# Attention and two MoE layers on one core: heads taken in pairs from the ninth unit on, the second batch's v sums moved to VectorE, and a re-costed planner

## The chip, the cores and the metric

The kernel runs on one core of one Trainium2 chip. The metric is the device time of one execution in microseconds (us), lower is better. An execution of this kernel is compared with another by the median of several runs; a profiled execution gives the trace.

## The reference

Inputs are q, k and v of shape (2 batches, 8 heads, 768 positions, 64) in float32, and four weight matrices in float64.

```python
k_sum = k.reshape(B, H, nb, block, D).max(axis=3)      # block = 32, so 24 blocks
v_sum = v.reshape(B, H, nb, block, D).mean(axis=3)
scores_l = scale * q @ k.T, kept where |i - j| < 16, else -1e9
scores_s = scale * q @ k_sum.T + log(32)
a = softmax(concat(scores_l, scores_s))                # a / (sum + 1e-9)
attn = a @ concat(v, v_sum)
x = attn as (1536 tokens, 512)
h = x @ w_in;  x = (h * clip(h + 3, 0, 6) / 6) @ w_out     # first MoE layer, 512 -> 2048 -> 512
h = x @ w_in2; out = (h * cos(h)) @ w_out2                 # second MoE layer
```

So each query sees at most 31 neighbours of its own and 24 block summaries, and the attention output is the token matrix of the first MoE layer. The host only lays the inputs out (transposed q and k with 16 columns of padding, v cut into windows of 96 rows).

## The kernel before, in words

**Attention.** A unit is one pair of heads (they share the 128 partitions, 64 each), one batch and 256 queries: `HT` = 2 tiles of 128. There are 24 units: 2 batches x 3 query thirds (`h`) x 4 pairs (`p`). A unit (`att`, L505) does the following. TensorE makes the scores in 8 small matmuls of 64x64 stationary elements (`score`, L515) into the two PSUM banks `s`, against a window of 96 keys and the 24 block maxima (120 columns, `CE`). VectorE adds the mask and takes the minimum in four instructions (L529), ScalarE takes four exponentials with their sums (L537), GpSimd adds 1e-9 (L546), VectorE inverts (L551) and GpSimd or VectorE scales (L555). TensorE transposes four 128x120 pieces into bank `t` (L564), ScalarE or VectorE copies them to `pt`, and TensorE multiplies by v in 8 small matmuls (`pv`, L573) into bank `o`. The result goes to SBUF as `xh` and the remainder `xl` (L580 and L582, by helpers at L403 and L410).

The k maxima are VectorE reductions (`k_prep`, L497). The v block means are made on TensorE: `vsum_pe` (L470) runs twelve matmuls of 96x32 stationary elements against the constant `avg` (L477), copies the bank to `y`, adds the four row groups with one more matmul (L482), copies the 24 rows to `vs`, and `fill` (L489) spreads them over the 12 windows of `vw`.

The score matmuls, the v product, and both matmuls of the v sums use tiles of the TensorE array (64x64, 120x64, 96x32, 128x32). All other matmuls, the transposes among them, use the array whole.

**MoE.** Weights arrive as float64 numbers, two 32-bit words each, and are unpacked by ScalarE, VectorE and GpSimd into a high and a low part (`weights`, L609). `g1` (L657) computes h for a chunk of 128 hidden columns: 3 matmuls for each of 4 slices of the model dimension (L667 to L669); `post` (L676) makes the activation with its high and low part; `g2` (L726) accumulates the output (L743). A block is 512 tokens and 4 chunks; the first block is cut into two halves of 256 tokens. In all there are 192 MoE matmuls of 256 columns and 2208 of 512.

**Who sets the order.** `Plan` (L121) is a list scheduler that runs when the kernel is built. Every operation has the engines that may do it with a cost on each, a priority, and what it reads, writes and takes. `order` (L243) plays the program with these costs, always gives a free engine the ready operation of lowest priority number, and so fixes the order on each of TensorE, ScalarE, VectorE, GpSimd and the one DMA queue of SyncE. On the chip these orders are fixed programs: an engine waits at an instruction until what it reads is there, with all later ones behind it. The planner's costs are never seen by the chip. Priorities come from the table `T` (L77): `A0` and `AS` set the start and spacing of the units, `g0` and `gi` those of the MoE chunks, and others move a load or a preparation ahead. `refine` (L223) repeats the plan with due times.

```python
    units += [(b, h, p) for b in range(B) for h in range(NH) for p in range(NP) if b or h > 1]
    for y, (b, h, p) in enumerate(units):
        pr = A0 + AS * HT * y
        ...
        att(b, h, p, kws[p], z, vws[p], pr, c_s)
```

Of the kernel before, what the change touches and what calls it, by code (L numbers as in the profile page):

```python
# [11 lines left out]
F32 = mybir.dt.float32  # L12
# [6 lines left out]
P = 128  # L19
# [28 lines left out]
def layout(q, k, v, moe_w_in, moe_w_out, moe2_w_in, moe2_w_out):  # L48
# [5 lines left out]
    qt, kt = (pair(x).transpose(0, 1, 2, 4, 3).reshape(B, NP, P, S) for x in (q, k))  # L54
# [5 lines left out]
    return dict(q=qt, k=kt, v=vw, w_in1=w_in[0], w_out1=w_out[0], w_in2=w_in[1], w_out2=w_out[1])  # L60


def consts():
# [14 lines left out]
    A0=6.982, AS=1.584, mask=-12.92, kp=-20.41, qp=-33.47, lk=-17.33, lq=-11.81, lv=-4.43, vs=33.64, vss=-16.92,  # L78
    vsp=-29.27, wl=-1.64, wc=-25.07, g0=20.77, gi=7.33, pp=27.42, fill=-9.73, DVE=1.348, POOL=0.497, cold=5, d0=0.9,
    warm=9, tail=1, lagq=1, nraw=3, ncf=2, n=5, w2=2, n2=3, g2=3, nz=3, busy=0, slack=0.2, vpe=-7.47, avg=-27.4,  # L80
# [36 lines left out]
class Op:  # L117
    __slots__ = ("engs", "fn", "prio", "port", "seq", "wait", "after", "ready", "takes", "uses", "start", "eng", "took")


class Plan:  # L121


    AFTER = {"PE": 0.2, "ACT": 0.135, "DVE": 0.13, "POOL": 0.09, "DMA": 0.95}
    TO_PE = {"PE": 0.0, "ACT": 0.2, "DVE": 0.19, "POOL": 0.15, "DMA": 0.95}
# [6 lines left out]
    def op(self, engs, fn, prio, r=(), w=(), take=(), port=0.0):  # L132
        o = Op()
        o.engs, o.fn, o.prio, o.port, o.seq = engs, fn, prio, port, len(self.ops)
# [49 lines left out]
    def deadlines(self, order):  # L184
# [17 lines left out]
        for o in reversed(order):  # L202
            t = end
            for a in o.after:
                t = min(t, late[id(a)] - (self.TO_PE if a.eng == "PE" else self.AFTER)[o.eng])
            for x in o.uses:
                if id(x) in follow and id(follow[id(x)]) in late:
                    t = min(t, late[id(follow[id(x)])] - self.AFTER[o.eng])
# [33 lines left out]

    def order(self):  # L243
# [5 lines left out]
        moved = self.end = 0.0  # L249
# [13 lines left out]
        while events:  # L263
# [11 lines left out]
            for e in names:  # L275
# [29 lines left out]
                cost = o.engs[e] * (2.0 if e == "PE" and now < T["cold"] else 1.0)  # L305
                if e == "DVE" and free["POOL"] > now + 0.1:
                    cost += o.port
# [3 lines left out]
                if e == "DMA":  # L311
                    moved = max(moved, now + 1.1) + cost
                    end, free[e] = moved, max(now + 0.52, moved - 2.5)
                    self.end = max(self.end, end + 1.3)
                else:
                    free[e] = end
                    self.end = max(self.end, end)
                push(free[e], "free", None)
                if o.seq < self.first:
                    first -= 1  # L320
                    opens = max(opens, end + self.AFTER[e])
                    if not first:
                        push(opens, "turn", None)
                for a in o.after:
                    a.ready = max(a.ready, end + (self.TO_PE if "PE" in a.engs else self.AFTER)[e])
# [3 lines left out]
                for x in o.uses:  # L329
                    x.uses -= 1  # L330
                    if not x.uses:
                        push(end + self.AFTER[e], "release", x)
# [4 lines left out]
    def run(self):  # L337
        self.refine()
        left, last, spare = self.first, T["cold"], True
        for o in self.order():  # L340
            if o.eng == "PE":
                if spare and last < T["busy"]:
                    for _ in range(int((o.start - last - T["slack"]) / (0.11 if last > T["cold"] else 0.22))):
                        self.idle()
                last = o.start + o.took
                spare = spare and not any(x.cls is self.spare and x.slot == 1 for x in o.uses)
# [8 lines left out]
def body(ctx: ExitStack, tc: tile.TileContext, q, k, v, w_in1, w_out1, w_in2, w_out2, ident_d, mask_d, avg_d, out):  # L355
# [13 lines left out]
    avg = ap.tile([P, AW + QD], F32, name="avg")  # L369
# [5 lines left out]
    part01 = [[cp.tile([P, TOK], F32, name=f"part{j}{m}") for m in range(KT)] for j in range(2)]  # L375
    c_z = slots("z", T["nz"], [P, HT * P], pool=ap)
    c_vw = slots("vw", 4, [P, NS, P], pool=ap)
    c_vs = slots("vs", 2, [P, P], pool=ap)
    c_y = slots("y", 1, [P, P], pool=ap)
# [53 lines left out]
    pl.spare = c_acc  # L433
    pl.idle = lambda: nc.tensor.matmul(out=c_acc.tiles[1][:, 0:SUB], lhsT=ident, rhs=ident[:, 0:SUB], start=True, stop=True)
# [6 lines left out]
    def load_consts():  # L441
        dma(lambda: mask[:, 1, :], lambda: mask_d, 0.34, T["mask"], w=["mask"])

# [9 lines left out]
    def load_q(b, h, p, prio):  # L453
        z = Buf(c_z)
        dma(lambda: z.t, lambda: q[b, p][:, HT * P * h:HT * P * h + HT * P], 0.54, prio, w=[z], take=[z])
        return z

    def load_k(b, p, prio):
# [3 lines left out]
            2.45, prio, w=[(kw, "own")], take=[kw])  # L462
        return kw, ks

    def load_v(b, p, prio):
        vw = Buf(c_vw)
        dma(lambda: vw.t[0:CW, :, :], lambda: v[b, p], 1.75, prio, w=[(vw, 0)], take=[vw])
        return vw

    def vsum_pe(vw, prio):  # L470

        bank, x, y = Buf(c_h), Buf(c_vs), Buf(c_y)

        def mm(e):
            for s in range(NS):
                a, g = 2 * (NS - 1 - s), s % 4 * QD
                nc.tensor.matmul(out=bank.t[g:g + QD, 0:P], lhsT=avg[0:CW, a:a + QD], rhs=vw.t[0:CW, s, :],  # L477
                                 start=(s < 4), stop=(s >= NS - 4), tile_position=(0, g))

        op({"PE": 0.85}, mm, prio, r=["avg", (vw, 0)], w=[bank], take=[bank, x, y])  # L480
        op({"ACT": 0.2, "DVE": 0.2}, lambda e: copy(e, y.t, bank.t[:, 0:P]), prio, r=[bank], w=[y])
        op({"PE": 0.25}, lambda e: nc.tensor.matmul(out=bank.t[CW:P, P:2 * P], lhsT=avg[:, AW:AW + QD], rhs=y.t,  # L482
# [341 lines left out]
```

## Time and profile before

| | |
|---|---|
| median of 3 runs | 609.16 us (608.8 to 609.82) |
| span of the profiled execution, first to last instruction | 605.7 us |
| what lies around the span, by the median | 3.5 us |
| TensorE (PE) busy | 590.8 us, 98% of the span |
| VectorE, ScalarE, GpSimd busy | 385.7, 268.5, 346.9 us (64%, 44%, 57%) |
| chain that ended last | PE 92%, all else 1 to 2% each |
| bytes read from HBM | 46.31 MB, mean 83 GB/s |

The page gives the span of the profiled execution and no separate end-to-end time, so the time of that execution is taken as its span and the 3.5 us around it. A busy share of PE counts each matmul from its start to its modelled end, and matmuls overlap; how fast PE really goes is read from the distance between the starts of its instructions in the timeline.

### The profile page before, as it was taken

The page shows a single profiled execution, that of the slowest core. Times are in us where ns is not written, and L with a number is a line of the kernel's source. Part 1 is how long each engine was busy: PE and PEld are TensorE (multiplying, and loading weights), DVE is VectorE, ACT ScalarE, POOL GpSimd, SP SyncE. Part 2 cuts the span into 40 slices and gives each one's busy share as a digit, 9 for nine tenths or more (in the row PEclk, how much of TensorE's full clock was granted, in tenths as well). Part 3 has the DMA queues.
Part 4 walks back from the last instruction along what each step waited for, and adds up shares of the span by engine and source line. Part 5 has one row for each costly group of instructions (what it writes and reads, how often), then busy time and mean ns, then how long its engine had stood idle before and what let it go on. Part 6 is the DMA issues. An engine that isn't in the chain of part 4 may idle for free.

```text
span 605.7 us, 9370 instructions
## 1 busy us (share of the span) xinstructions
PE 590.8 (98%) x3490; PEld 484.6 (80%) x3490; DVE 385.7 (64%) x724; ACT 268.5 (44%) x585; POOL 346.9 (57%) x366
## 2 busy tenths in 40 slices
PE   5889999999999999999999999999999999999997
PEld 4568787788888888888888888888888888888886
DVE  3699994433942259523982689857984897574562
ACT  3788896533421214201440546654662363343240
POOL 2677774645843537524688398655863577443340
PEclk9999999999999999999999999999999999999999
DMA  9979940122410014200530013302330030000112
GB/s 229 291 232 296 249 137 12 35 105 70 139 70 0 1 42 149 90 0 1 170 108 0 1 70 106 104 2 73 101 104 2 0 105 0 2 0 1 70 44 95
DMA packets 28333, 50.05 MB, mean 83 GB/s; under 512 B 14464, under 2 KB 17920, under 8 KB 28288
## 3 DMA queue, kind: packets, MB, share of 16 engines
q1 hardware_dynamic: 28144, 49.40, 26.9%
q8 instruction: 27, 0.44, 0.3%
q14 instruction: 18, 0.15, 0.1%
q10 hardware_dynamic: 144, 0.07, 0.0%
HBM read 46.31 MB, written 3.15 MB: 82 GB/s over the span
## 4 chain that ended last, share of the span: by engine, by line
PE 92%; DVE 2%; POOL 2%; DMA 1%; ACT 1%; issue 1%; SPq 0%; DVEq 0%; POOLq 0%; ACTq 0%
PE acc L743 25%; PE s L743 18%; PE h L667 8%; PE h L668 8%; PE h L669 8%; PE o L668 3%; PE t L668 3%; PE o L669 3%; PE t L669 3%; PE t L667 3%; PE o L667 3%; PE s L515 2%; PE t L564 2%; PE o L573 2%; DVE cf L627 1%; DMA z<-in_q_dram 1%
## 5 line engine op out<-in xcount | busy, mean ns | idle before, releaser
L405 POOL TENSOR_SCALAR g<-r 128x512 fp32r<-128x512 f32 (+1 forms) x81 | 61.9, 764 | 135.4 <-DVE r L703 40.7
L410 POOL TENSOR_TENSOR g<-r,g 128x512 fp32r<-128x512 f32 (+1 forms) x73 | 100.5, 1377 | 7.3 <-ACT g L403 2.8
L699 ACT ACTIVATE n<-h,bias 128x512 f32<-128x512 f32 (+1 forms) x60 | 39.4, 656 | 142.1 <-PE h L669 140.0
L743 PE MATMUL acc<-g,w 128*128 128x512 f32 (+1 forms) x432 | 96.1, 370 | 0.0
L667 PE MATMUL h<-xh,w 128*128 128x512 f32 (+1 forms) x240 | 92.4, 385 | 0.0
L668 PE MATMUL h<-xl,w 128*128 128x512 f32 (+1 forms) x240 | 90.1, 375 | 0.6 <-DVE xl L410 0.6
L669 PE MATMUL h<-xh,w 128*128 128x512 f32 (+1 forms) x240 | 89.9, 375 | 0.0
L743 PEld LDWEIGHTS acc<-g,w 128*128 128x128 f32 x432 | 75.3, 188 | 14.3 <-issue 0.8
L703 DVE SCALAR_TENSOR_TENSOR r<-n,h 128x512 f32<-128x512 f32 (+1 forms) x60 | 38.7, 646 | 56.8 <-ACT n L699 31.1
L743 PE MATMUL acc<-w,g 128*128 128x512 f32 x288 | 69.2, 389 | 0.0
L743 PE MATMUL s<-w,g 128*128 128x512 f32 x288 | 69.2, 389 | 0.0
L410 POOL TENSOR_TENSOR w<-cf,w 128x512 fp32r<-128x512 f32 x44 | 63.9, 1456 | 3.3 <-ACT w L403 1.6
L743 PEld LDWEIGHTS acc<-w,g 128*128 128x128 f32 x288 | 54.1, 188 | 11.2
L743 PEld LDWEIGHTS s<-w,g 128*128 128x128 f32 x288 | 54.0, 188 | 11.2
L627 DVE SCALAR_TENSOR_TENSOR cf<-cu,cf 128x512 uint32<-128x512 uint32 x64 | 60.0, 955 | 0.4
L618 ACT ACTIVATE cu<-raw 128x512 f32<-128x512 f32 x64 | 42.9, 670 | 38.2 <-DVE cf L627 23.6
L622 DVE TENSOR_SCALAR cf<-raw 128x512 uint32<-128x512 uint32 x64 | 46.6, 744 | 11.8 <-POOL w L410 11.6
L667 PEld LDWEIGHTS h<-xh,w 128*128 128x128 f32 x240 | 45.1, 188 | 10.0 <-issue 1.7
L711 POOL TENSOR_SCALAR n<-n 128x512 f32<-128x512 f32 x45 | 31.5, 700 | 37.6 <-ACT n L699 37.6
L668 PEld LDWEIGHTS h<-xl,w 128*128 128x128 f32 x240 | 45.1, 188 | 8.5 <-DVE xl L410 0.8
L669 PEld LDWEIGHTS h<-xh,w 128*128 128x128 f32 x240 | 45.1, 188 | 8.2
L405 POOL TENSOR_SCALAR w<-cf 128x512 fp32r<-128x512 f32 x41 | 31.4, 771 | 30.3 <-DVE cf L627 23.2
(93 smaller groups left out, 1025.9 us busy)
## 6 DMA issues: line engine op xcount, KB each, us to landing
raw<-in_w_in_dram SPq DMA_DIRECT2D x32, 512.0 KB, 4.1
raw<-in_w_out_dram SPq DMA_DIRECT2D x32, 512.0 KB, 3.8
kw<-in_k_dram SPq DMA_DIRECT2D x8, 576.0 KB, 5.7
vw<-in_v_dram SPq DMA_DIRECT2D x8, 576.0 KB, 9.0
z<-in_q_dram SPq DMA_DIRECT2D x24, 128.0 KB, 5.9
out_dram<-part SPq DMA_DIRECT2D x8, 256.0 KB, 2.0
out_dram<-kw SPq DMA_DIRECT2D x3, 256.0 KB, 2.0
out_dram<-kw SPq DMA_DIRECT2D x2, 128.0 KB, 1.7
```

The lines of the kernel that those rows point to most:

```text
L405: eng[e].tensor_scalar(out=out, in0=in_, scalar1=scale, scalar2=0.0, op0=ALU.mult, op1=ALU.add)
L410: eng[e].tensor_tensor(out=out, in0=in0, in1=in1.bitcast(F32), op=ALU.subtract)
L618: lambda e, raw=raw, u=u: nc.scalar.activation(out=u.t, in_=raw.t.bitcast(F32)[:, :, 1], func=ACTF.Prelu, scale=2.0 ** -112, alpha=2.0 ** 32),
L622: lambda e, raw=raw, f=f: eng[e].tensor_scalar(out=f.t.bitcast(U32), in0=raw.t[:, :, 0], scalar1=2.0 ** -29, scalar2=7.0, op0=ALU.mult, op ...
L627: lambda e, u=u, f=f: nc.vector.scalar_tensor_tensor(out=f.t.bitcast(U32), in0=u.t.bitcast(U32), scalar=3, in1=f.t.bitcast(U32), op0=ALU.l ...
L667: nc.tensor.matmul(out=o, lhsT=wh, rhs=hi, start=(kk == 0), stop=False)
L668: nc.tensor.matmul(out=o, lhsT=wh, rhs=lo, start=False, stop=False)
L669: nc.tensor.matmul(out=o, lhsT=wl, rhs=hi, start=False, stop=(kk == KT - 1))
L699: op({"ACT": t(fixed, 0.43)}, lambda e: nc.scalar.activation(out=out(), in_=in_(), func=func, **kw), pr, r=rd, w=wr, take=take)
L703: op({"DVE": t(0.09, 0.56)}, lambda e: nc.vector.scalar_tensor_tensor(out=out(), in0=a(), scalar=s, in1=b(), op0=o0, op1=o1), pr, r=rd, w= ...
L711: op({"POOL": t(0.16, 0.47), "DVE": t(0.07, 0.265)}, lambda e: eng[e].tensor_scalar(out=n(), in0=n(), scalar1=1.0, scalar2=-MAGIC, op0=ALU ...
L743: nc.tensor.matmul(out=o, lhsT=l, rhs=r, start=(c == 0 and z == 0), stop=(c == GS - 1 and z == 2))
```

## The change

Four things are changed.

1. **Pairs.** The units of the last third of batch 0 and all of batch 1 (from the ninth unit on) are taken two pairs of heads at a time: eight double units. One score run makes the scores of both (16 small matmuls in a row, columns 0 to 239 and 240 to 479 of the same two banks), the softmax and transposes stay one pair at a time, and one `pv` run multiplies both by v, with one `xh` and one `xl` evacuation of twice the width.
2. **v sums of batch 1.** The host also passes v transposed (`vt`). For batch 1 it is loaded into `y` (128x768), VectorE sums groups of 32 (new `tensor_reduce`), TensorE transposes the 24 columns back, and the copy to `vs` scales by 1/32. The twelve matmuls and the one after them are gone for these four pairs; batch 0 keeps them.
3. **Planner.** Costs are changed; an entry into a tiled mode costs 0.15 more, a PE operation that was only just ready costs more, PE costs double while a modelled clock is slow, and VectorE and GpSimd delay each other by a modelled lock. A new step `nudge` moves priorities at random, with 25 fixed seeds.
4. **The table `T`.** Among others A0 from 6.982 to -22.127, AS from 1.584 to 1.369, g0 from 20.77 to 40.246, gi from 7.33 to 11.932 and pp from 27.42 to 80.856.

```diff
+NUDGES = (301016, 301018, ...)
-            op({"PE": 0.58}, score, prio,
+        op({"PE": 0.17 + 0.4 * n}, score, prio, mode=1,
-    def vsum_pe(vw, prio):
+    def v_sums(b, p, prio):
         bank, x, y = Buf(c_h), Buf(c_vs), Buf(c_y)
+        if b:
+            dma(lambda: y.t, lambda: vf[b - 1, p], 1.15, prio + T["lvt"], w=[y], take=[y])
+            op({"DVE": 0.86},
+               lambda e: nc.vector.tensor_reduce(
+                   out=x.t[:, CW:CE], in_=y.t.rearrange("p (c j) -> p c j", j=BLK), axis=AX.X, op=ALU.add),
+               prio, r=[y], w=[(x, 2)], take=[x])
+            op({"PE": 0.11}, lambda e: nc.tensor.transpose(out=bank.t[0:CE, 0:P], in_=x.t[:, 0:CE], identity=ident),
+               prio, r=[(x, 2)], w=[bank], take=[bank])
+            op({"ACT": 0.172, "DVE": 0.215}, lambda e: copy(e, x.t[CW:CE, :], bank.t[CW:CE, 0:P], 1.0 / BLK), prio,
+               r=[bank], w=[(x, 0), (x, 1), (x, 2)])
+            return x
...
         def score(e):
+            for x, p in enumerate(ps):
+                for i, u, o in subs:
+                    nc.tensor.matmul(
+                        out=sp[o].t[u * SUB:u * SUB + SUB, x * W + i * CE:x * W + i * CE + CE], ...)
...
         def pv(e):
+            for x, p in enumerate(ps):
+                for i, u, o in subs:
+                    f = slice(D * o, D * o + D)
+                    a, c = (2 * i + o) * P + u * SUB, (x * HT + i) * P + u * SUB
+                    nc.tensor.matmul(out=res.t[f, c:c + SUB], lhsT=vws[b, p].t[0:CE, 2 * (HT * h + i) + u, f],
+                                     rhs=pts[x].t[0:CE, a:a + SUB], start=True, stop=True)
...
-    units += [(b, h, p) for b in range(B) for h in range(NH) for p in range(NP) if b or h > 1]
+    units = [(b, h, (p,)) for b, h, p in units]
+    units += [(b, h, (p, p + 1)) for b in range(B) for h in range(NH) for p in range(0, NP, 2) if b or h > 1]
...
+    for x in c_vs.tiles:
+        nc.gpsimd.memset(x, 0.0)
...
+                if e == "PE":
+                    while tick_at <= now:
+                        slow, busy, tick_at = self.clock(slow, busy), 0.0, tick_at + self.WATCH
+                    cost *= 2.0 if slow else 1.0
+                    if o.mode and not mode:
+                        cost += 0.15
```

What this does to the order on the engines is shown at three places. The first is TensorE in the middle of the attention, where the v sums of batch 1 stand. Before (`avg` marks the v sums, `pt` the v product, `ident` the transposes, the rest is MoE):

```order
L743 MATMUL acc_130<-g_126,w_116 128x256 x3
L477 MATMUL h_133<-vw_89,avg 32x128 x12
L564 MATMUL t_134<-ident,e_102 120x128 x4
L667 MATMUL h_132<-xh_69,w_119 128x256
L668 MATMUL h_132<-xl_72,w_119 128x256
L669 MATMUL h_132<-xh_69,w_119 128x256
L482 MATMUL h_133<-y_93,avg 32x128
L573 MATMUL o_135<-pt_108,vw_88 64x64 x8
```

And now, with the line numbers of the changed kernel, one transpose of `vs` in the same stage:

```order
L813 MATMUL acc_130<-g_126,w_116 128x256 x3
L514 MATMUL h_132<-ident,vs_91 120x128
L813 MATMUL acc_130<-g_127,w_117 128x256 x3
L813 MATMUL acc_130<-g_128,w_118 128x256 x3
L813 MATMUL acc_131<-g_126,w_116 128x256 x3
L580 MATMUL t_134<-ident,e_100 120x128 x4
```

Two tiled runs among whole-array work have become one whole-array transpose.

The second place is the v product of units 15 and 16 on TensorE now. Before, each such run stood alone, as the last row of the first piece does:

```order
L737 MATMUL h_132<-xh_69,w_117 128x512
L738 MATMUL h_132<-xl_72,w_117 128x512
L739 MATMUL h_132<-xh_69,w_117 128x512
L591 MATMUL o_135<-pt_107,vw_89 64x64 x8
L591 MATMUL o_135<-pt_108,vw_90 64x64 x8
L813 MATMUL acc_130<-g_126,w_116 128x256 x3
L580 MATMUL t_134<-ident,e_101 120x128 x4
```

Two v products follow each other without whole-array work between them.

The third place is the queue of SyncE where the v windows of batch 1 are loaded (`vw`; `z` is q, `raw` a weight chunk, `y` the transposed v). Before:

```order
L437 DMA raw_111<-in_w_out_dram 128x1024
L437 DMA z_86<-in_q_dram 128x256
L437 DMA vw_87<-in_v_dram 96x1536
L437 DMA z_84<-in_q_dram 128x256
L437 DMA vw_88<-in_v_dram 96x1536
L437 DMA z_85<-in_q_dram 128x256
L437 DMA vw_89<-in_v_dram 96x1536
L437 DMA vw_90<-in_v_dram 96x1536
```

Now:

```order
L474 DMA z_85<-in_q_dram 128x256
L474 DMA raw_111<-in_w_in_dram 128x1024
L474 DMA vw_87<-in_v_dram 96x1536
L474 DMA vw_88<-in_v_dram 96x1536
L474 DMA vw_89<-in_v_dram 96x1536
L474 DMA y_93<-in_vt_dram 128x768
L474 DMA vw_90<-in_v_dram 96x1536
L474 DMA raw_109<-in_w_out_dram 128x1024
```

The second v window stands as the 44th load in both, with two of the four `y` loads ahead of it now (they stand as the 25th and 33rd).

## Rows read from the trace of the kernel before

**Rows 1.** Busy time by stretch (us; per engine busy and count; PEclk is the granted clock).
```profile
core 0: us, PE busy (x) PEld busy (x) DVE busy (x) ACT busy (x) POOL busy (x), PEclk, DMA share, GB/s
0.00:32.10 32.10, 22.44 (x292) 16.59 (x292) 16.90 (x83) 17.79 (x64) 15.20 (x27) 1.00 1.01 261
32.10:123.30 91.20, 89.48 (x1090) 71.77 (x1087) 69.83 (x248) 70.67 (x237) 63.17 (x76) 1.00 0.56 160
123.30:605.70 482.40, 478.91 (x2113) 396.21 (x2111) 298.99 (x395) 180.09 (x284) 268.49 (x264) 1.00 0.17 56
```

**Rows 2.** Timeline of PE (start, duration, operation), start of the unbroken MoE stretch.
```profile
123.33 0.39 PE L667 MATMUL h<-xh,w 128*128 128x512 f32 x1
123.56 0.39 PE L668 MATMUL h<-xl,w 128*128 128x512 f32 x1
```

**Rows 3.** Timeline of PE, a v sum, a score run and MoE between them.
```profile
66.79 0.86 PE L477 MATMUL h<-vw,avg 96*32 96x128 f32 x24
67.58 0.64 PE L515 MATMUL s<-kw,z 64*64 64x120 f32 x16
68.15 0.39 PE L667 MATMUL h<-xh,w 128*128 128x256 f32 x1
68.38 0.28 PE L668 MATMUL h<-xl,w 128*128 128x256 f32 x1
68.50 0.28 PE L669 MATMUL h<-xh,w 128*128 128x256 f32 x1
68.70 0.41 PE L482 MATMUL h<-y,avg 128*32 128x128 f32 x2
69.04 0.39 PE L667 MATMUL h<-xh,w 128*128 128x256 f32 x1
```

**Rows 4.** Timeline of PE, transposes and what follows them.
```profile
63.65 0.60 PE L564 MATMUL t<-ident,e 128*120 128x128 f32 x4
64.00 0.95 PE L743 MATMUL acc<-g,w 128*128 128x256 f32 x6
```

**Rows 5.** Timeline of PE, v products of units 13 and 24 and a follower.
```profile
72.19 0.69 PE L573 MATMUL o<-pt,vw 120*64 120x64 f32 x16
72.81 0.61 PE L743 MATMUL acc<-g,w 128*128 128x256 f32 x3
...
114.41 0.69 PE L573 MATMUL o<-pt,vw 120*64 120x64 f32 x16
```

**Rows 6.** Timeline of PEld, weight loads of a score run and a v product.
```profile
67.58 0.41 PEld L515 LDWEIGHTS s<-kw,z 64*64 64x64 f32 x16 [0.20 <-DVE xl L410]
...
72.19 0.55 PEld L573 LDWEIGHTS o<-pt,vw 120*64 120x64 f32 x16 [0.20 <-issue]
```

**Rows 7.** Timeline of PE, transposes early and later, v product of unit 6.
```profile
14.41 1.11 PE L564 MATMUL t<-ident,e 128*120 128x128 f32 x4
...
22.59 0.65 PE L564 MATMUL t<-ident,e 128*120 128x128 f32 x4
...
38.11 0.69 PE L573 MATMUL o<-pt,vw 120*64 120x64 f32 x16
```

**Rows 8.** Timeline of ACT, last exponentials of units 6 and 14.
```profile
30.66 0.39 ACT L537 ACTIVATE e<-e,sm 128x120 f32<-128x120 f32 x1
...
63.30 0.38 ACT L537 ACTIVATE e<-e,sm 128x120 f32<-128x120 f32 x1
```

**Rows 9.** Busy time between those two, columns as in the first group.
```profile
31.00:63.70 32.70, 30.79 (x421) 25.62 (x420) 30.63 (x116) 28.64 (x101) 25.32 (x33) 1.00 0.89 260
```

**Rows 10.** VectorE groups, 31 to 63.7 us (count, busy us, mean ns, idle before).
```profile
L627 DVE SCALAR_TENSOR_TENSOR cf<-cu,cf 128x512 uint32<-128x512 uint32 x7 | 7.6, 1094 | 0.0
L497 DVE TENSOR_REDUCE ks<-kw 128x12 f32<-128x384 f32 x8 | 4.1, 541 | 0.0
L410 DVE TENSOR_TENSOR g<-r,g 128x256 fp32r<-128x256 f32 x3 | 2.4, 785 | 0.0
```

**Rows 11.** Queue of SP: second v window of batch 1; time to landing.
```profile
57.91 0.42 SPq L437 DMA_DIRECT2D vw<-in_v_dram  x1
...
vw<-in_v_dram SPq DMA_DIRECT2D x8, 576.0 KB, 9.0
```

More of the change, by code (lines that the diff above doesn't have):

```diff
@@ L2 @@
 import math
+import random
 from contextlib import ExitStack
@@ L117 @@
 class Op:
-    __slots__ = ("engs", "fn", "prio", "port", "seq", "wait", "after", "ready", "takes", "uses", "start", "eng", "took")
+    __slots__ = ("engs", "fn", "prio", "port", "mode", "seq", "wait", "after", "ready", "takes", "uses", "start", "eng", "took")
 class Plan:
-    AFTER = {"PE": 0.2, "ACT": 0.135, "DVE": 0.13, "POOL": 0.09, "DMA": 0.95}
-    TO_PE = {"PE": 0.0, "ACT": 0.2, "DVE": 0.19, "POOL": 0.15, "DMA": 0.95}
+    OUT = {"PE": 0.165, "ACT": 0.097, "DVE": 0.081, "POOL": 0.04, "DMA": 0.05}
+    IN = {"PE": 0.06, "ACT": 0.035, "DVE": 0.035, "POOL": 0.085, "DMA": 0.06}
     LOAD = {"PE": 1.0, "ACT": 1.0, "DVE": T["DVE"], "POOL": T["POOL"], "DMA": 1.0}
@@ L241, in refine, with clock, nudge @@
         self.reset()
+    WATCH = 3.413
+    def clock(self, slow, busy):
+        share = busy / self.WATCH
+        return share < 0.93 if slow else share < 0.55
+    def nudge(self):
+        self.order()
+        at = [o.start for o in self.ops]
+        self.reset()
+        for seed in NUDGES:
+            r = random.Random(seed)
+            c, w, g, f = r.uniform(-5, 115), r.choice((1, 3, 8, 25)), r.choice((0.1, 0.3, 1, 3)), r.choice((0.1, 0.4, 1))
+            for t, o in zip(at, self.ops):
+                if abs(t - c) < w and r.random() < f:
+                    o.prio += r.gauss(0, g)
     def order(self):
@@ L248, in order @@
         tick = 0
-        moved = self.end = 0.0
+        moved = self.end = held = busy = 0.0
+        mode, slow, tick_at = 0, True, 1.5
         free["DMA"] = T["d0"]
@@ L311, in order @@
                 if e == "DMA":
-                    moved = max(moved, now + 1.1) + cost
-                    end, free[e] = moved, max(now + 0.52, moved - 2.5)
+                    moved = max(moved, now + 2.0) + cost
+                    end, free[e] = moved, max(now + 0.45, moved - 4.5)
                     self.end = max(self.end, end + 1.3)
@@ L338, in run @@
         self.refine()
-        left, last, spare = self.first, T["cold"], True
+        self.nudge()
+        left = self.first
         for o in self.order():
[L341 to L346, printed above, removed]
             o.fn(o.eng)
@@ L461, in load_k @@
             lambda: bass.AP(tensor=k.tensor, offset=k.offset + (b * NP + p) * P * SP, ap=[[SP, P], [SUB, NS], [1, CW]]),
-            2.45, prio, w=[(kw, "own")], take=[kw])
+            2.2, prio, w=[(kw, "own")], take=[kw])
         return kw, ks
```

221 lines of the change are left out of this document (122 added, 99 removed).

## The prediction

> **What bounds the kernel now.** I read the busy time by stretch first [rows 1]. From 123.3 us to the end PE is busy for 478.91 of 482.40 us. Inside, one 512-column matmul starts 0.23 us after the other [rows 2], and the order there is the same pattern of whole blocks before and after the change. So this stretch moves as a block: whatever happens is decided by when PE gets through the attention and the first 288 MoE matmuls that share PE with it. That is what the reader is to see in the first group: a rate-bound end, and a first part in which PE had other things to wait for.
>
> Then I price that first part from the timeline, always from a start to the next start. A twelve-matmul v sum takes 67.58 - 66.79 = 0.79 us, a score run 68.15 - 67.58 = 0.57, the matmul after a v sum 69.04 - 68.70 = 0.34 [rows 3], four transposes 0.35 to 0.36 [rows 4], a v product 72.81 - 72.19 = 0.62 [rows 5]. A half-width MoE matmul takes 68.50 - 68.38 = 0.12, and yet three of them between two tiled runs take 68.70 - 68.15 = 0.55 instead of 0.36 [rows 3]. So each stay of PE in a tiled mode costs its whole-array neighbours about 0.19 us, once going in and once coming out.
>
> With these prices PE's work in the first 123.3 us is: MoE 192 x 0.12 + 96 x 0.227 = 44.8; 24 score runs 13.7; 24 v products 14.9; 24 transposes 8.6; eight v sums 6.3 and their second matmuls 2.7; 36 stays in a tiled mode behind the first MoE matmul (counted in the order) x 0.19 = 6.8. Together 97.8. The remaining 25.5 us PE waits or runs at half speed: 20.4 of it before the first MoE matmul at 32.1 us (that part holds 11.7 us of work), 5.1 after it. **Two numbers decide: the work that the change removes from PE, and what becomes of the 25.5.**
>
> **The work that goes.** *v sums of batch 1.* Four times 0.79 + 0.34 = 4.5 go, four single transposes of about 0.36 / 4 = 0.09 come: -4.1 us. The reduction that takes their place on VectorE is not in the trace; twice 128x384 at 541 ns [rows 10] bounds it above at 1.08 us, once bounds it below at 0.54. I take 1.0, four times, of which one falls before unit 14 and three later, with VectorE busy for 69.83 of 91.2 us in all [rows 1]; it is covered there. Without that cover it would cost up to 4.3 us. The copies to `y` go, those to `vs` stay.
>
> *Stays in a tiled mode.* In the order after the first MoE matmul they fall from 36 to 13: 23 x 0.19 = -4.4 us. *The runs themselves.* The 16 weight loads of a score run take 0.41 of its 0.57 us [rows 6], and the rest lies before the next load. A second run in the same mode can start loading at once, so it costs between 0.41 and 0.57; I take 0.41. For the v product it is 0.55 against 0.62 by the same reading. Eight times 0.16 + 0.07 = -1.8 us, with zero as the other bound. Sum: **-10.3 us** of PE work (-8.5 to -10.3).
>
> The rows show that a v sum takes the same step before a score run in another tiled shape [rows 3] as before transposes, so I price no change from one tiled shape to another. The Trainium skill (TensorEngine Tiling (Array Packing), Key Properties) says that a change of the tiling mode drains the engine, not of a tile within it. By that rule the direct tiled-to-tiled changes, which fall from 11 to 4, would give up to another 0.7 us; the trace agrees for tiled against whole-array and shows nothing of it between tiled shapes.
>
> *Small edits.* The double-width evacuations save one fixed part each on ScalarE and VectorE; the two memsets stand on GpSimd before any data has landed; both at nothing. The four `y` loads are 4 x 0.39 = 1.6 MB. At the 261 GB/s of the first stretch [rows 1] that is 6 us of DMA, hidden from 32 us on, where the DMA share is 0.56, but not free in the queue up to 60 us (see the rivals). The changed costs act only through the order.
>
> **What becomes of the waits.** The new order brings the attention forward. Before the first MoE matmul it has 10 score runs, 6 v products, 6 transposes and all 4 v sums of batch 0 (before: 7, 4, 5 and 3), in all 16.0 us of work. The last of these is the v product of unit 6, so that unit dates the start. Its last exponential now ends at 31.0 [rows 8] and its v product runs at 38.1 [rows 7]. There weight instructions stand ahead of it, four on ScalarE alone; in the new order neither ScalarE nor VectorE has one ahead of unit 6. The fourth window of k is about 5 MB into the queue, at 261 GB/s some 20 us and with the lag of the queue 22. Two reductions of 0.54, copy, score run and exponentials take about 5 us more: **27 us instead of 31**. With the same 7.1 us to the v product, MoE starts at **34 us**, and 34 - 16.0 = 18.0 us are waits.
>
> From there to the v products of units 13 and 14 PE is short of work: the order gives it only 78 half-width MoE matmuls (9.4), six score runs, eight transposes, six v products and five stays, 19.9 us in all. The softmax sets the pace. In before, units 7 to 14 take 32.7 us, in which VectorE is busy for 30.63 and ScalarE for 28.64 [rows 9]. Counted in the order, VectorE then does 57 attention and 14 weight and MoE instructions (before 57 and 23): two weight combinations of 1.09, three `g` remainders of 0.79 [rows 10] and four cheaper ones go, about 5.8 us less. ScalarE does 29 beside the exponentials (before 35), about 2.9 less. So ScalarE has 25.7 us to do; at the 88% that it reached, 29 us. Unit 14's exponentials end at 27 + 29 = 56, and with some 6 us to the v product (as unit 6 took 7.1) that runs at **62 us**. It waits for the copies of both pairs, and on PE all MoE behind it waits with it. Waits there: 62 - 34 - 19.9 = 8.1. From then on 102 MoE matmuls stand before the next v product, and PE has work; I allow 2 us. Total waits 18.0 + 8.1 + 2 = 28.1 against 25.5: **+2.6**.
>
> **Sum.** -10.3 + 2.6 = -7.7 us: span 598.0, and with the 3.5 us that lie around the span of before by the median, **601.5 us**. The profiled execution has no end-to-end time of its own, so this stands against the median, 609.16.
>
> **Rivals.**
> *A, slower: v of batch 1 comes late.* In before its second window is issued at 57.91 us and takes about 9 us [rows 11]; unit 13's v product runs at 72.19 [rows 5]. Now the first v product of batch 1 needs the windows of both pairs at once, and two `y` loads stand ahead in the queue (0.8 MB, 3 us). If the queue is as late as before, the double product runs between 70 (58 + 9 + 3) and 75 (72.2 + 3), say 74. The work up to it is 16.0 + 19.9 = 35.9, so 38.1 us are waits, with 2 later +14.6 against -10.3: **613.5 us**. It decides for slower where that product runs later than about 70 us (35.9 + 25.5 + 10.3 - 2). Against it: the windows were issued that late since the slots of `vw` and `raw` came free late, and their users run earlier now.
>
> *B, the clock.* At 14.41 us four transposes take 1.11 us, at 22.59 0.65 [rows 7]: PE starts out at the lower of its levels, although the granted clock of the stretch reads 1.00 [rows 1]. Between 34 and 62 us PE now works 20 of 28 us with short waits. If half of that runs at the low level, it costs some 7 us, of which waits cover a part: **606 us**. Against: in before nothing after 22 us shows the longer step, with waits of the same kind between. The Trainium skill (TensorE: Matmul & The Clock Gate, A second HAM failure mode: psum-queue depth-cycling) tells of a kernel that swung between both levels as PE idled briefly between groups; by that rule this rival would hold. The trace of before does not show it after 22 us.
>
> *C, the drains turn into waits.* VectorE and ScalarE do nearly the same work up to unit 24 as before. If they set its v product (before at 114.41 [rows 5], with the same 252 MoE matmuls ahead in both orders), only the earlier start of unit 6 is left, 4 us: **605.5 us**. Against: their busy time leaves 21 of 91 us [rows 1].
>
> **How the numbers follow.** My forecast has 0.66, C 0.14, B 0.10, A 0.10. Range: with waits as before and 1.5 us better, 597.5; above it reaches past B and C to 607.0 and leaves out A. A measurement of this kernel can tell about 0.2% (1.2 us) from no change. Faster by more: all of the forecast, most of B and C, 0.87; within: 0.05; slower: 0.08.
>
> **What would show it.** Right: 13 stays in a tiled mode; no v sum in batch 1; first MoE matmul near 34 us; the double v product of units 13 and 14 near 62 with waits between; the unbroken stretch from about 115 us, still 0.23 us a matmul. Wrong: a v product of batch 1 that waits for a DMA beyond 70 us (A), transposes of 1.1 us after 25 us (B), or waits for exponentials after unit 14 (C).

## The result and the profile after

The changed kernel takes 603.38 us (median of 4 runs, 602.58 to 605.06) against 608.98 of the kernel before (4 runs, 607.62 to 609.82): ratio 0.9919, 95% interval 0.9895 to 0.9943, so 5.6 us faster. The forecast was 601.5 us, with a range of 597.5 to 607.0. The profiled execution took 603.37 us with a span of 601.5. In the runs of both kernels 1.8 to 2 us lie around the span; so the profiled execution of before, with its span of 605.7, took about 607.5 and lay 1.5 us below its median. By the spans the gain is 4.2 us, and the two figures differ by less than the interval of the ratio (1.5 us either way).

Busy time by stretch of the changed kernel, cut at its first MoE matmul, at the v product of units 13 and 14, and where equally many MoE matmuls are done as at 123.3 us before. It answers to [rows 1, 9].

```profile
core 0: us, PE busy (x) PEld busy (x) DVE busy (x) ACT busy (x) POOL busy (x), PEclk, DMA share, GB/s
0.00:36.50 36.50, 24.19 (x402) 18.25 (x402) 18.57 (x101) 20.34 (x77) 17.66 (x32) 1.00 1.00 255
36.50:66.20 29.70, 23.71 (x309) 20.77 (x304) 29.21 (x105) 27.36 (x95) 25.98 (x32) 0.94 1.01 284
66.20:118.60 52.40, 52.36 (x573) 45.06 (x573) 41.52 (x120) 36.39 (x117) 37.41 (x45) 1.00 0.38 129
```

PE waits in the first two rows and hardly in the third. From 118.6 us on a matmul still starts every 0.23 us, as in [rows 2]; 482.9 us follow, 482.4 before. So everything was decided in the first 118.6 us, 4.7 us fewer than before.

The timeline of PE, which answers to [rows 3, 5, 7]:

```profile
35.93 0.69 PE L591 MATMUL o<-pt,vw 120*64 120x64 f32 x16 [1.04 <-POOL sm L634]
36.55 0.39 PE L737 MATMUL h<-xh,w 128*128 128x256 f32 x1
...
61.81 0.42 PE L739 MATMUL h<-xh,w 128*128 128x256 f32 x1
62.02 0.41 PE L737 MATMUL h<-xh,w 128*128 128x256 f32 x1
...
66.24 1.15 PE L591 MATMUL o<-pt,vw 120*64 120x64 f32 x32
...
84.86 1.15 PE L591 MATMUL o<-pt,vw 120*64 120x64 f32 x32
...
89.15 1.05 PE L566 MATMUL s<-kw,z 64*64 64x120 f32 x32
90.13 1.15 PE L591 MATMUL o<-pt,vw 120*64 120x64 f32 x32
91.21 0.98 PE L813 MATMUL acc<-g,w 128*128 128x256 f32 x6
```

The first MoE matmul runs at 36.55 us (forecast 34), the double v product of units 13 and 14 at 66.24 (62). A double score run takes 90.13 - 89.15 = 0.98 us, as taken (0.57 + 0.41); a double v product 91.21 - 90.13 = 1.08 instead of 1.17. Around 62 us a half-width matmul takes 0.21 us instead of 0.12: PE is at the lower level there.

The three longest waits of PE between 36.5 and 67 us (us in total, times, longest):

```profile
PE t L580 <- POOL e L643: 3.0, 3, 1.1
PE o L591 <- DVE xl L447: 1.1, 1, 1.1
PE s L566 <- DVE sm L617: 1.1, 1, 1.1
```

All three wait for VectorE and GpSimd at their work on the units before; none waits for a DMA. The new reduction, in a list of its instructions (count, least, median and largest ns, first and last start), takes 0.94 us, near the 1.0 taken:

```profile
L511 DVE TENSOR_REDUCE vs<-y x4: 940/943/947, 37.3 to 79.6; 128x24 f32<-128x768 f32 x4
```

### The profile page after: what moved, and what is told of

It is laid out like the page before. It is cut to its first block, busy times and chain, and to the rows that moved or that the text cites. A ratio compares the mean times of both kernels' runs of the same rounds, so it can differ in the third digit from the quotient of the medians.

```text
span 601.5 us, 9149 instructions
## 1 busy us (share of the span) xinstructions
PE 579.4 (96%) x3390; PEld 480.7 (80%) x3390; DVE 383.3 (64%) x711; ACT 262.0 (44%) x565; POOL 359.7 (60%) x385
## 4 chain that ended last, share of the span: by engine, by line
PE 90%; DMA 3%; DVE 2%; POOL 2%; SPq 1%; ACT 1%; issue 1%; DVEq 0%; POOLq 0%
PE acc L813 26%; PE s L813 18%; PE h L737 8%; PE h L739 8%; PE h L738 8%; PE o L738 3%; PE t L738 3%; PE t L739 3%; PE o L737 3%; PE o L739 3%; PE t L737 3%; DMA kw<-in_k_dram 2%; PE o L591 1%; DMA raw<-in_w_in_dram 1%; SPq L474 1%; PE t L580 1%
## 5 line engine op out<-in xcount | busy, mean ns | idle before, releaser
L447 POOL TENSOR_TENSOR g<-r,g 128x512 fp32r<-128x512 f32 (+1 forms) x85 | 111.7, 1316 | 4.7 <-ACT g L440 0.5
L447 POOL TENSOR_TENSOR w<-cf,w 128x512 fp32r<-128x512 f32 x46 | 67.3, 1466 | 1.4 <-ACT w L440 0.2
L697 DVE SCALAR_TENSOR_TENSOR cf<-cu,cf 128x512 uint32<-128x512 uint32 x64 | 61.8, 979 | 1.9 <-ACT cu L688 1.6
L442 POOL TENSOR_SCALAR w<-cf 128x512 fp32r<-128x512 f32 x43 | 31.9, 748 | 24.7 <-DVE cf L697 16.6
```

Of the source, the lines that this page charges most:

```text
L442: eng[e].tensor_scalar(out=out, in0=in_, scalar1=scale, scalar2=0.0, op0=ALU.mult, op1=ALU.add)
L447: eng[e].tensor_tensor(out=out, in0=in0, in1=in1.bitcast(F32), op=ALU.subtract)
L697: lambda e, u=u, f=f: nc.vector.scalar_tensor_tensor(out=f.t.bitcast(U32), in0=u.t.bitcast(U32), scalar=3, in1=f.t.bitcast(U32), op0=ALU.l ...
```

## The experiments

Times are medians; the ratio to the kernel before follows in brackets with its interval. The change itself stands at 603.38. Each ratio is to executions of the kernel before taken in the same session (medians 608.45 to 608.98). By these intervals a difference between two of the kernels below carries about 2 us either way, so a difference of 2.0 is at the edge of what the medians show, and the traces have to bear it out.

**What PE's work is worth.** Cut double runs (`o1_split`): each of ten double runs gets the next whole-array operation between its halves.

```diff
-            o.fn(o.eng)
...
+            if o.parts is not None:
+                o.parts("PE", (0,))
+                late = o
+            else:
+                o.fn(o.eng)
+                if late is not None and o.eng == "PE":
+                    late.parts("PE", (1,))
...
```

> The changed kernel with its planned order kept; ten of the double runs (two score runs and six v products behind 66 us, two score runs before it) are cut in two by the next whole-array operation on PE. Theory 1 (PE's work is paid for at its measured price once PE has no waits, behind 66 us): a cut costs 0.19 us for the extra stay in the tiled mode and 0.16 us for the run itself; the eight late cuts cost 8 x 0.35 = 2.8 us, the two early ones are mostly hidden in waits: 605.5 to 607 us against 603.4 of the changed kernel. Rival (changes of the mode cost nothing that lasts, and the gain came from the new order alone): within 0.5 us of the changed kernel.

606.42 us [0.9973, 0.9954 to 0.9992], 3.0 us more than the change (2.0 by the spans of the two profiles). The trace bears the price out: between the v products that run at 85.28 and 111.08 us here, and at 84.86 and 109.40 in the change, lie four of the cuts, and the stretch is 25.80 - 24.54 = 1.26 us longer, 0.31 us a cut against 0.35 expected.

The old work of the v sums beside the new (`o2_oldsums`): at each transpose of `vs` PE also runs twelve tiled matmuls and one more on constants.

```diff
...
+                for s in range(NS):
+                    a, g = 2 * (NS - 1 - s), s % 4 * QD
+                    nc.tensor.matmul(out=bank.t[g:g + QD, P:2 * P], lhsT=ident[0:CW, a:a + QD], ...)
...
```

> The changed kernel with its planned order kept; at each of the four transposes of batch 1's v sums, PE also runs twelve tiled matmuls before it and one behind it, as the v sums of before did, on constants and into columns that nobody reads. Theory 1 (what PE saves counts only behind 66 us, before that it becomes waiting): the two early ones (at 38.8 and 58.8 us) are hidden, the two late ones (71.8 and 81.0) cost 1.13 + 2 x 0.19 = 1.5 us each: +3.0 us, about 606.4 us. Theory 2 (all work that PE saved counts): +6 us, 609.4 us.

605.35 us [0.9957, 0.9936 to 0.9978], 2.0 more, and 2.0 by the spans. Its first MoE matmul and its v products of units 13 to 16:

```profile
36.83 0.39 PE L745 MATMUL h<-xh,w 128*128 128x256 f32 x1
...
65.55 1.15 PE L599 MATMUL o<-pt,vw 120*64 120x64 f32 x32
...
86.87 1.15 PE L599 MATMUL o<-pt,vw 120*64 120x64 f32 x32
```

Set against the run of the same order without a period at the lower level (`o7_halfv` below: 36.15, 64.58 and 84.17 us), and counted from the first MoE matmul, the v product of units 13 and 14 runs only 0.3 us later, though two of the four sums (2.3 us) stand before it; that of units 15 and 16 is 2.0 us later. So the early work went into PE's waits and the late work counted. Of the 6 us at which Theory 2 prices the whole of it, 2.0 show in the time.

**What sets the pace from 36 to 66 us.** A short `y` load (`o3_shorty`): of `vt` only 96 of 768 columns are loaded, so the v sums of batch 1 are wrong in part and 1.4 MB leave the queue.

```diff
-    for x in c_vs.tiles:
+    for x in (*c_vs.tiles, *c_y.tiles):
...
-            dma(lambda: y.t, lambda: vf[b - 1, p], 1.15, ...)
+            dma(lambda: y.t[:, 0:CW], lambda: vf[b - 1, p][:, 0:CW], 1.15, ...)
```

> The changed kernel with its planned order kept; each load of transposed v brings 96 of 768 columns (the other columns stay zero, so the v sums of batch 1 are not the right ones). It takes 4 x 0.34 MB from the queue, two of the four ahead of the weights of the fourth chunk and of v of batch 1. Theory A (the DMA queue, full until 66 us, sets when PE gets its work between 36 and 66 us): 0.7 MB at 284 GB/s less ahead, the v products of units 13 and 14 some 1.5 to 2.5 us earlier, 601 to 602 us. Theory B (VectorE and ScalarE, busy for 98% and 92% of that stretch, set the pace): the v product moves by less than 0.5 us and the time stays within 0.5 us of the changed kernel.

604.99 us [0.9942, 0.9919 to 0.9965]; the v product at 65.6 us. The queue of the change is full there (share 1.01), and taking 1.4 MB from it gains nothing: Theory A falls. Neither figure of Theory B came as written. The time is 1.6 us above the change, which the medians do not tell from nothing, and the product is 0.7 us earlier; the period at the lower level stands elsewhere in this profile (see the last section).

Each new reduction twice (`o5_tworeduce`):

```diff
-               lambda e: nc.vector.tensor_reduce(...),
+               lambda e: [nc.vector.tensor_reduce(...) for _ in range(2)],
```

> The changed kernel with its planned order kept; VectorE makes each of the four new reductions twice. Theory B (VectorE sets the pace between 36 and 66 us): the two reductions that stand before unit 14 cost their 0.9 us each, +1.8 us at the v product of units 13 and 14 and 1.2 to 2 us in the end, 604.6 to 605.4 us. Theory A (the DMA queue sets it): VectorE's extra time falls into its own waits, less than 0.5 us in the end.

605.38 us [0.9958, 0.9937 to 0.9978], 2.0 more; the first MoE matmul at 37.36 us, the v products of units 13 to 16 at 66.53 and 86.96. Its stretches:

```profile
60.00:70.00 10.00, 8.89 (x90) 7.95 (x90) 10.00 (x31) 8.06 (x28) 7.70 (x9) 1.00 1.01 228
...
80.00:90.00 10.00, 9.03 (x108) 7.47 (x107) 9.97 (x26) 6.92 (x23) 7.13 (x9) 1.00 0.57 185
```

VectorE (third of the busy times) is full in both, PE (first) is not. The first MoE matmul is 0.8 us later than in the change, before any added reduction (the first pair starts at 38.0 us), so that part is not theirs. Counted from the first MoE matmul and against `o7_halfv`, two more reductions of 0.94 us make the first of these products 0.7 us later, and all four the second 1.6: less than half their length. VectorE is no free cover, and it does not set the pace alone either.

**What makes the head long.** Half of batch 0's v (`o7_halfv`).

```diff
+    for x in c_vw.tiles:
+        nc.vector.memset(x[0:CW, NS // 2:, :], 0.0)
...
-        dma(lambda: vw.t[0:CW, :, :], lambda: v[b, p], 2.45, ...)
+        m = NS if b else NS // 2
+        dma(lambda: vw.t[0:CW, 0:m, :], lambda: v[b, p][:, 0:m], 2.45, ...)
```

> The changed kernel with only the first 6 of 12 windows of v loaded for batch 0 (four loads of half the size; the other half is set to zero at the start, so half of batch 0's v is left out of the computation). 1.2 MB, about 4.5 us of DMA at 261 GB/s, go from the first 36 us. Theory D (the first MoE matmul is late because the fourth window of k lands at 25.3 us in a DMA queue that is full from the start): that landing comes 2 to 4 us earlier, the first MoE matmul at 33 to 35 us instead of 36.5, the end 1.5 to 3 us earlier (600.5 to 602). Rival (the chain of scores, exponentials and copies of the first six units sets it): the landing is earlier but the first MoE matmul stays within 0.8 us of 36.5, and the end within 1 us.

602.09 us [0.9892, 0.9865 to 0.9919]. The loads of k in this kernel, the issue of the fourth and the time to landing (least, median, largest):

```profile
14.37 0.43 SPq L476 DMA_DIRECT2D kw<-in_k_dram  x1
...
DMA to landing us min/median/max: 5.1/6.7/7.5
```

Its timeline, and its first stretch:

```profile
24.45 0.18 DVE L642 RECIPROCAL sm<-sm 128x4 f32<-128x4 f32 x1 [0.20 <-POOL sm L637]
24.55 0.98 DVE L546 TENSOR_REDUCE ks<-kw 128x12 f32<-128x384 f32 x2
...
35.53 0.69 PE L594 MATMUL o<-pt,vw 120*64 120x64 f32 x16
36.15 0.39 PE L740 MATMUL h<-xh,w 128*128 128x256 f32 x1
...
64.58 1.15 PE L594 MATMUL o<-pt,vw 120*64 120x64 f32 x32
```

```profile
0.00:36.10 36.10, 25.49 (x402) 18.90 (x402) 22.76 (x105) 20.36 (x77) 17.28 (x32) 0.86 0.82 224
```

The same in the changed kernel:

```profile
25.36 1.01 DVE L543 TENSOR_REDUCE ks<-kw 128x12 f32<-128x384 f32 x2 [0.58 <-DMA kw<-in_k_dram]
```

The fourth window of k lands at 14.4 + 5.1 = 19.5 us instead of 25.3, the DMA share falls from 1.00 to 0.82, and the first MoE matmul comes only 0.4 us earlier. The reduction stands on VectorE behind a reciprocal that waits for GpSimd, which adds 1e-9 to sums that wait for the exponentials of a unit before. Theory D falls for this landing: a full queue and a late landing were there, but the chain through five engines in fixed order takes nearly as long without them. (The added memsets, 1.1 to 4.2 us on VectorE, stand ahead of its first reduction, which runs at 8.2 us instead of 7.9; they do not hide an effect of 2 us.) The end lies between both expectations, and 1.3 us by the medians is within what two kernels differ by. By the profiles the span is 0.7 us shorter: 0.4 are from the head, and 0.3 are what is left of the period at the lower level that the change has near 62 us and this profile has not.

**What the order is worth.** Both visible parts taken back (`a3_planner`):

```diff
-        if b:
+        if b > 1:
...
-    units += [(b, h, (p, p + 1)) ... for p in range(0, NP, 2) if b or h > 1]
+    units += [(b, h, (p,)) ... for p in range(NP) if b or h > 1]
```

> The changed kernel with both visible parts taken back: all units single, the v sums of batch 1 on TensorE as before; the new planner and table order this program, with 28 stays in a tiled mode behind the first MoE matmul (before 36, after 13). Theory (TensorE's work plus its waits): the v sums (4.1 us) and the run bodies (2.6 us) come back, of the stays only 8 x 0.19 = 1.5 us are saved, and the planner alone has no power over the softmax: 607 to 612 us, no faster than before by more than 2 us. Rival (the planner's order by itself is what gains): 604 us or less.

611.59 us [1.0034, 1.0011 to 1.0058]. Only the pairs taken back (`a1_nopairs`, the second of these edits alone):

> The changed kernel with all units single; the v sums of batch 1 stay on VectorE; new planner and table, 30 stays in a tiled mode behind the first MoE matmul. PE's work grows by 17 x 0.19 + 2.6 = 5.8 us against the change. Both taken back cost 611.6 us. Theory (PE's work counts, and shorter waits of the singles give a part back): 605.5 to 609 us, so that each visible part holds about half of the gain. Rival (the pairs cost in waits what they save in work): within 1.5 us of the changed kernel, 602 to 605 us.

608.94 us [1.0003, 0.9982 to 1.0024]. The visible parts with the old planner and table (`a5_oldplan`; the costs of the single operations stay those of the change):

```diff
-    A0=-22.127, AS=1.369, ...
+    A0=6.982, AS=1.584, ...
...
-                    if o.mode and not mode:
-                        cost += 0.15
```

> The two visible parts (double units, v sums of batch 1 on VectorE) with the planner's rules and the table of before: 17 stays in a tiled mode behind the first MoE matmul. Theory (work plus waits): the work falls by 4.1 + 19 x 0.19 + 2.6 = 10.3 us, nearly as in the change, and the weight instructions that the old order puts ahead of the softmax cost waits of the size of before or a little more: 599 to 603 us, as good as the change or better. Rival (without the new order the double units wait for their second pair and give the work back in waits): 605 us or more.

610.96 us [1.0043, 1.0023 to 1.0062]. The rival's number came; its mechanism, a wait for the second pair, is not what the longest wait shows, since unit 7 is still a single unit. The timeline where the v product of unit 7 waits, PE and then VectorE:

```profile
49.65 1.12 PE L556 MATMUL o<-pt,vw 120*64 120x64 f32 x16 [3.16 <-DVE xl L411]
...
47.28 0.43 DVE L657 TENSOR_SCALAR cf<-raw 128x512 uint32<-128x512 uint32 x1 [1.16 <-POOL w L411]
47.63 0.68 DVE L662 SCALAR_TENSOR_TENSOR cf<-cu,cf 128x512 uint32<-128x512 uint32 x1
48.23 0.94 DVE L476 TENSOR_REDUCE vs<-y 128x24 f32<-128x768 f32 x1
49.09 0.41 DVE L411 TENSOR_TENSOR xl<-o,xh 128x256 fp32r<-128x256 f32 x1
```

Two weight instructions and the new reduction stand on VectorE ahead of the `xl` that frees the bank. PE is busy for 41.45 of 50.2 us between its first MoE matmul (34.8) and the v product of units 13 and 14, which runs at 85.0 us. Part of the loss is of another kind: between 48 and 54.5 us PE is at the lower level in this profile.

| us | old planner and table | new |
|---|---|---|
| neither visible part | 608.98 | 611.59 |
| VectorE sums alone | not run | 608.94 |
| both | 610.96 | 603.38 |

With the new order the two parts are worth 8.2 us (pairs 5.6, sums 2.7), with the old one they lose 2.0, and the new order alone loses 2.6. The parts do not add. These differences hold for the tables as they are: no mixed kernel got a table of its own, so what the parts or the new rules would give with one is not shown.

Then the planner's rules and its table apart (`a6_newrules`: new rules without random shifts, old table; `a7_newtable`: old rules, new table), each by a part of the edits of `a5_oldplan`.

> The two visible parts with the planner's new rules (without random shifts) and the table of before; 18 stays in a tiled mode behind the first MoE matmul. The kernel with old rules and old table took 610.96 us. Theory R (the rules see the cost of a stay and of a late operation, and so make the order that gains): 602 to 605 us. Theory T (the table with its earlier start of the units makes it): 608 to 612 us, with the double product of units 13 and 14 later than 75 us.

> The two visible parts with the planner's rules of before and the new table; 14 stays in a tiled mode behind the first MoE matmul, and the last v product stands behind 147 MoE matmuls instead of 237. Theory T (the table makes the gain): 602 to 606 us, with the double product of units 13 and 14 by 68 us. Theory R (the rules make it): 608 us or more; the attention then runs ahead with little MoE beside it, and the waits before its end grow past 40 us.

610.89 us [1.0032, 1.0011 to 1.0053] and 619.24 us [1.0174, 1.0148 to 1.0201]. Each kernel came out as the theory against it said, so neither the rules nor the table gains by itself; that a table fitted to the rules is what they need is argued, not shown. In `a7_newtable` the last v product runs at 100.0 us, earlier than in the change (109.4), and the span is 15 us longer: an early end of the attention is worth nothing if MoE did not run beside it. The clock has a part in these losses too. After 20 us PE is at the lower level for some 7 us in the profile of `a5_oldplan`, 20 in `a6_newrules` and 14 in `a7_newtable`, against 3.4 in the change and none in the kernel before; how much of the loss is waits and how much the clock, no run separates.

Without random shifts (`a4_nonudge`):

```diff
-        for seed in NUDGES:
+        for seed in ():
```

> The changed kernel without the random shifts of priorities; 13 stays in a tiled mode as in the change. Theory (the time is set by the stays, the first landing of k and the pace of the softmax, which small shifts of the order do not alter): within 1.5 us of the changed kernel, 602 to 605 us. Rival (the shifts were chosen for an order that avoids waits): 605.5 us or more, with the difference visible as waits before 120 us.

602.79 us [0.992, 0.9895 to 0.9946]: the shifts are worth nothing that these runs can tell.

**A try at a better version** (`c1_mixed`):

```diff
-        if b:
+        if b and p > 1:
```

> A try at a better version, without random shifts: in batch 1 the v sums of the first two pairs of heads go back to TensorE and only the last two stay on VectorE. Two reductions of 0.94 us leave VectorE before 66 us; TensorE gets 2 x (0.79 + 0.34 - 0.09) + 4 x 0.19 = 2.8 us of work there. Theory B (VectorE sets the pace from 36 to 66 us, and TensorE's early work lies in its waits): 1 us faster than the change without random shifts, 601.5 to 603. Rival (TensorE's work counts wherever it stands): 2 to 3 us slower, 605 to 606.

605.55 us [0.9956, 0.9934 to 0.9979], 2.8 slower than `a4_nonudge` (1.8 by the spans). The number is the rival's. The dates in this kernel, for the first two pairs of batch 1:

```profile
61.21 0.86 PE L523 MATMUL h<-vw,avg 96*32 96x128 f32 x24
64.27 0.86 PE L523 MATMUL h<-vw,avg 96*32 96x128 f32 x24
68.80 0.69 PE L591 MATMUL o<-pt,vw 120*64 120x64 f32 x16
...
65.62 1.80 POOL L442 TENSOR_SCALAR vw<-vs 24x1536 f32<-24x1536 f32 x1
```

And without this edit (`a4_nonudge`; duration, first and last start):

```profile
L442 POOL TENSOR_SCALAR vw<-vs x2: 1473/1640/1808, 53.6 to 60.8; 24x1536 f32<-24x1536 f32 x2
```

A v sum on PE needs the v windows, of which the first land about 60 us, and sum, copies and fill (`vw`) follow one after the other: the v product runs at 68.8 instead of 64.4 us. It does not follow that this chain costs the time. The stretches from the first MoE matmul to that v product, this kernel first and then `a4_nonudge` (length, then PE's busy time):

```profile
36.30:68.80 32.50, 28.29 (x369) 23.29 (x367) 31.47 (x113) 29.45 (x103) 29.34 (x38) 0.95 1.06 279
...
36.30:64.40 28.10, 22.13 (x307) 18.99 (x303) 27.81 (x97) 26.41 (x91) 24.82 (x29) 1.00 1.05 292
```

PE stands idle for 32.50 - 28.29 = 4.2 us here and for 28.10 - 22.13 = 6.0 there, and up to the unbroken stretch for 4.4 against 6.8 in all. It waits less, and is slower by the work put back (2.8 us by the prices) and by a period at the lower level between 48 and 52 us. That is the rival's reading, with a part of the work taken up by waits, as in `o2_oldsums`. In the change the transposed copies are issued from 31.6 us on, and the sums of these two pairs are ready by about 60 us; that this by itself gains time is not shown.

No version beat the change by more than the measurement tells; the one without random shifts does as well with less.

## Why the prediction was right, and which terms failed

The time came inside the range, 1.9 us above the forecast: the work was right, the waits were put too low by 3.8 us.

*What bounds the kernel* held: the steady end kept its length, and all was decided before 118.6 us.

*The work that goes* (-10.3) held: a cut of a run costs 0.31 us in the trace against 0.35 (`o1_split`), and the sum by the rows after is -11.0; PE's busy time fell from 590.8 to 579.4 us. The mis-sized term is the second v product: the pair takes 1.08, so a body saves 0.16 instead of 0.07. Work removed is not time gained, though: of the v sums' work put back, only a part showed (`o2_oldsums`).

*What becomes of the waits* (+2.6) was mis-sized: the same working gives 36.55 - 16.0 = 20.5 before the first MoE matmul (18.0 forecast), 66.24 - 36.55 - 19.9 = 9.8 up to the v product (8.1), and some 1.6 later (2), together 31.9 against 25.5: **+6.4**. Of the miss, 2.5 us lie in the first term. Of the 1.7 in the second, 1.3 come with the period at the lower level: in `o7_halfv`, which has none there, that stretch takes 64.58 - 36.15 = 28.4 us, against 28 forecast and 29.7 here. Two steps failed, one in its size and one in its reason.

The first is the date of unit 6. Its last exponential ended at 30.4 us instead of 27, as the fourth window of k landed at 25.3 and not at 22. But `o7_halfv` shows that the landing was not the reason: with 19.5 us the first MoE matmul was at 36.15. I took the chain from the landing alone and left out what stands ahead on VectorE and ScalarE. After the exponentials, too, other work stands in ScalarE's order ahead of unit 6's copy: weight instructions, exponentials of unit 7 and a copy to `xh` (its timeline in the change):

```profile
30.35 0.66 ACT L688 ACTIVATE cu<-raw 128x512 f32<-128x512 f32 x1
...
32.59 0.68 ACT L688 ACTIVATE cu<-raw 128x512 f32<-128x512 f32 x1
33.18 0.61 ACT L440 ACTIVATE w<-cf 128x512 fp32r<-128x512 f32 x1
33.70 0.38 ACT L625 ACTIVATE e<-e,sm 128x120 f32<-128x120 f32 x1
...
34.95 0.38 ACT L440 ACTIVATE xh<-o 128x256 fp32r<-128x256 f32 x1
35.23 0.59 ACT L440 ACTIVATE pt<-t 120x512 f32<-120x512 f32 x1
```

My sentence that no weight instruction stands ahead of unit 6 does not hold for this copy, two us after its transposes. Moving it up was not tried, so what each of these instructions adds to the 2.5 us stays open.

The second is what sets the pace to 62 us. The length came out, the reason did not: I gave the pace to ScalarE at 88%, and VectorE was busy for 29.21 of 29.70 us, yet 1.9 us more for VectorE moved the v product by 0.7 only (`o5_tworeduce`), so no single engine sets it. "Covered there" was wrong too: the reductions, put at nothing, cost up to half their length.

Rival B came true for one stretch. In the change and in `a4_nonudge` PE does the same work here, after similar waits:

```profile
60.57 1.01 PE L580 MATMUL t<-ident,e 128*120 128x128 f32 x4
...
62.66 1.48 PE L813 MATMUL acc<-g,w 128*128 128x256 f32 x6
63.94 0.35 PE L737 MATMUL h<-xh,w 128*128 128x256 f32 x1
```

```profile
60.21 0.62 PE L580 MATMUL t<-ident,e 128*120 128x128 f32 x4
...
61.39 0.88 PE L813 MATMUL acc<-g,w 128*128 128x256 f32 x6
62.10 0.28 PE L737 MATMUL h<-xh,w 128*128 128x256 f32 x1
```

63.94 - 60.57 = 3.37 us at the lower level (1.2 GHz) against 62.10 - 60.21 = 1.89 at the higher (2.4 GHz): 1.5 us, not the 4.5 of the rival. Little of it stays: from the first MoE matmul to the v product of units 15 and 16 the change takes 84.86 - 36.55 = 48.3 us and `o7_halfv` 84.17 - 36.15 = 48.0, since PE waits less afterwards.

*Sum.* -11.0 + 6.4 = -4.6 us of span, with 0.5 more in the steady end -4.1; measured were -4.2 by the spans, and -5.6 by the medians, against -7.7 forecast. This agreement is bookkeeping: the waits are what is left of the time when the priced work is taken off, so the sum has to come near the span; the prices are tested by `o1_split`, not by it. What I put around the span, 3.5 us, is 1.8 to 2; the rest was the 1.5 us by which the profiled execution of before lay under its median, so a sum made against the median was right to hold it. From the forecast to the measured median it is 601.5 - 0.7 (work) + 3.8 (waits) + 0.5 (steady end) - 1.7 (around the span) = 603.4 us: the last term hides a part of the second, which is luck.

*Rivals.* A fell: the first v product of batch 1 ran at 66.24 us, 3.8 before its deciding point, with no wait for a DMA. C fell: after 66.2 us PE is busy for 52.36 of 52.40. What failed in the list is what it left out: the waits were worked out for the new order, but no rival asked what the two parts do without it ("The changed costs act only through the order"). With the same two parts, planner and table decide between 603.4 and 611.0.

## What to carry to other kernels

Where engines run fixed orders, price a change to the work and the order that goes with it as one: here each alone, with tables not fitted to it, lost 2 to 3 us and together they gained 5.6. To date a stage, follow the last input through every instruction that stands ahead of it on each engine; a transfer that lands last need not be what the stage waits for. A saving on the bottleneck engine counts only where that engine does not wait. And before a slower try is put down to a later date of one stage, compare how long the bottleneck engine stood idle in both.

## What the runs showed of the hardware

The place of the lower clock level is not fixed by the program. With nearly the same order of PE up to 66 us the granted clock lay at the lower level between 61 and 64 us in the change, between 26 and 30 us in `o1_split`, between 41 and 44 in `o3_shorty`, and nowhere after 20 us in `o2_oldsums`, `o5_tworeduce`, `a4_nonudge` and `o7_halfv`. Near 62 us it made 1.9 us of work take 3.4, and by 85 us 0.3 of the 1.5 us lost was left. The Trainium skill (TensorE: Matmul & The Clock Gate, A second HAM failure mode: psum-queue depth-cycling) tells of such swings after brief idling; the traces agree that they occur, and add that the same idling often passes without one. The mean granted clock of the four executions of the change ran from 0.982 to 0.996, so one profile is no measure of what the lower level takes.

VectorE can be slowed by GpSimd, but is not always. In `a5_oldplan` the same VectorE instruction on a 128x512 weight took 1.71 us while GpSimd filled `vw`, and 0.43 at 47.28 us (shown above) while GpSimd was idle:

```profile
40.92 1.81 POOL L406 TENSOR_SCALAR vw<-vs 24x1536 f32<-24x1536 f32 x1
...
41.30 1.71 DVE L657 TENSOR_SCALAR cf<-raw 128x512 uint32<-128x512 uint32 x1
...
45.69 1.56 POOL L411 TENSOR_TENSOR w<-cf,w 128x512 fp32r<-128x512 f32 x1 [1.29 <-ACT w L404]
...
45.71 0.41 DVE L657 TENSOR_SCALAR cf<-raw 128x512 uint32<-128x512 uint32 x1
```

At 45.71 us it took 0.41 beside another GpSimd instruction that had just started. The Trainium skill (Perfetto Trace Analysis, Optimizing Scalar/DVE Operations) says that the two share a read port, which an operation of VectorE can hold alone; the rows agree with a wait of that kind, at 41.30 us on VectorE's side.
